# A threshold-attention and MoE kernel: one batch's q and k turned by TensorE instead of the DMA, and the output tiles of the drain spread over three PSUM buffers

## Chip, cores and metric

The kernel runs on one core of one Trainium2 chip. The metric is device time in microseconds for one launch: the median of several runs, beside one profiled execution whose trace gives every duration below.

## What is computed

Attention over 8 batches, 8 heads, 576 positions and head dimension 64, with a threshold: only scores within tau = 0.02 of the row's maximum survive. Its output, 4608 tokens of 512, goes through a two-layer network with a leaky ReLU.

```python
scores = scale * np.matmul(q, k.transpose(0, 1, 3, 2))
thresh = np.max(scores, axis=-1, keepdims=True) - tau
scores = np.where(scores >= thresh, scores, -1000000000.0)
attn = np.exp(scores - np.max(scores, axis=-1, keepdims=True))
attn = attn / (np.sum(attn, axis=-1, keepdims=True) + 1e-09)
x = np.matmul(attn, v)                       # then (batch, seq, heads * dim)
h = x @ w_in                                 # 512 -> 2048
out = np.maximum(0.01 * h, h) @ w_out        # 2048 -> 512
```

All inputs and the output are float32.

## The kernel before

**Splitting.** Scores need more than half precision, so q and k, scaled by 64, are each split into a high and a low fp16 part (`hi` on ScalarE, `x64` and `lo` on POOL), and three products are summed in PSUM. A batch's four pairs of heads are handled in two halves, `hb` 0 and 1. A tile `ks` or `qs` holds both parts of a half, positions on the partitions, as 18 blocks of 128x128; scores need it with the head dimension on the partitions, as `kst` or `qst`. There are two ways to turn it. `turn` is one DMA transpose on SyncE's queue. `turn_pe` lets TensorE transpose block by block through an identity into a PSUM tile named `tp`, which ScalarE or VectorE copies to `kst` or `qst`. Before the change, batch 0 takes `turn_pe` and the other seven take `turn`: 28 DMA transposes.

**Steps.** The main loop has one score step for 128 query rows of one pair of heads: 18 steps for a batch. In a step TensorE computes scores of two heads (`scores`, tags `sc0` and `sc1`, one buffer of two banks each). VectorE scales them into `sf` and takes the row maximum (line 391, `smax`), POOL makes the bias `bb` from it and applies it to one head (lines 515 and 517), ScalarE to the other (516). One step later VectorE cuts at the threshold (546), and ScalarE takes the exponential into `w` with its row sum (551). Two steps make a unit; one step after its last exponential VectorE adds the reciprocal sums to `w` (534, 536) and SyncE issues a DMA transpose `wt` of it (540). Seven steps after the unit's last score step TensorE multiplies `wt` with v (`pv`, 362) and VectorE writes the scaled result to `xT` (372, 378).

**The network.** When a group's `xT` is complete (two blocks of 128 tokens as a rule, for the first group after step 14) its work is put in queues: `h_unit` makes the hidden units with 8 or 16 matmuls into a PSUM tile `hp` (tag `h`, two buffers of a bank), ScalarE applies a ReLU scaled by 0.99, and a step later VectorE adds 0.01 of `hp` (`leak`, 216). `o_unit` sums 4 output matmuls at a time into `op` (tag `o`, one buffer). After 16 of them `op` is copied to `osb` and stored. One hidden and one output unit are taken per step. After the last step a loop, the drain, takes what is left in turn.

**Order.** Each engine runs its instructions in the order in which the code emits them. What is not part of a step (loads, splitting, turning) is put into the lists `tick` and `ptick` by step number and is emitted at the end of that step. [...] `sc0` and `sc1` two banks each, `h` two, `o` and `pv` one each. The calls that place the turns, and the tile that the drain uses:

```python
at(t0 + 4, lambda b=b, hb=hb: turn("k", b, hb))   # t0 = 4 for the first half of batch 1
at(t0 + 7, lambda b=b, hb=hb: turn("q", b, hb))
...
G.op = ps.tile([128, 512], FP32, tag="o", bufs=1, name="op")
```

Of the kernel before, what the change touches and what calls it, by code (L numbers as in the profile page):

```python
# [9 lines left out]
FP32 = mybir.dt.float32  # L10
# [6 lines left out]
def kernel(  # L17
# [42 lines left out]
    WOUT = 0  # L60
    SPOOL = 5
    LOADS = (-4, 3)

    sb = ctx.enter_context(tc.tile_pool(name="sb", bufs=1))
    ps = ctx.enter_context(tc.tile_pool(name="ps", bufs=1, space=bass.MemoryType.PSUM))
# [27 lines left out]
    def load_half(src, store, nm, b, hb):  # L93

        m = store[b, hb] = sb.tile([128, 2, 576], FP32, tag=nm, bufs=2, name=nm)
        in_ = src[b, :, :, :].rearrange("(h f) (p t) d -> f p h (t d)", h=2, t=9)[ds(2 * hb, 2)]
        if nm == "km":
            nc.sync.dma_start(out=m, in_=in_.rearrange("f p h x -> (f p) h x"))  # L100
        else:
            for f in range(2):
                nc.sync.dma_start(out=m.rearrange("(p f) h x -> f p h x", f=2)[f], in_=in_[f])
# [3 lines left out]
    def after_anchor(ins):  # L107

        if anchor[0] is not None:
            tc.add_manual_dep(  # L110
                ins.ins, anchor[0].ins.name,
                mybir.DependencyInfo(mybir.DependencyClass.Sync, mybir.DependencyReason.DATA), reason="port")

    def load_v(b, i):

        if i == 0:
            vts[b] = vbufs[b % 2]
        vt = vts[b]
        sv = v[b, :, :, :].rearrange("(h g) (p t) d -> h p g (t d)", h=2, t=9)
        out_, in_ = [  # L120
            (vt[0:64, :, 0, 0:5, :], sv[0][:, :, 0:320]),
            (vt[64:128, :, 0, 0:4, :], sv[0][:, :, 320:576]),
            (vt[64:128, :, 1, 0:5, :], sv[1][:, :, 0:320]),
            (vt[0:64, :, 1, 1:5, :], sv[1][:, :, 320:576]),
        ][i]
        after_anchor(nc.gpsimd.dma_start(out=out_, in_=in_))  # L126
# [5 lines left out]
    def split_tile(nm, b, hb):  # L132
        store = kss if nm == "k" else qss
        if (b, hb) not in store:
            store[b, hb] = sb.tile([128, 2, 9, 2, 64], FP16, tag=nm + "s", bufs=2, name=nm + "s")
        return store[b, hb]
# [14 lines left out]
    def hi(nm, b, hb):  # L151
        for part in PARTS[nm]:
            src, dst = views(nm, b, hb, 0, part)
            hi_last[0] = nc.scalar.activation(out=dst, in_=src, func=AF.Copy, bias=0.0, scale=64.0)

    def x64(nm, b, hb, h):
        m = (kms if nm == "k" else qms)[b, hb][:, h, :]
        return nc.gpsimd.tensor_scalar(out=m, in0=m, scalar1=64.0, scalar2=1.0, op0=AX.mult, op1=AX.mult)

    def lo(nm, b, hb, h, part, eng="pool"):  # L160
        src, dst = views(nm, b, hb, 1, part)
        _, h_ = views(nm, b, hb, 0, part)
        if eng == "pool":
            return nc.gpsimd.tensor_tensor(out=dst[:, h], in0=src[:, h], in1=h_[:, h], op=AX.subtract)  # L164
        return nc.vector.scalar_tensor_tensor(
            out=dst[:, h], in0=src[:, h], scalar=64.0, in1=h_[:, h], op0=AX.mult, op1=AX.subtract)

    def turned(nm, b, hb):

        store = ksts if nm == "k" else qsts  # L170
        if (b, hb) not in store:
            store[b, hb] = sb.tile([128, 2, 9, 2, 64], FP16, tag=nm + "st", bufs=4, name=nm + "st")
        return store[b, hb]

    def turn(nm, b, hb):
        nc.sync.dma_start(
            out=turned(nm, b, hb).rearrange("p s t g r -> p (s t) (g r)"),
            in_=split_tile(nm, b, hb).rearrange("p s t h d -> p (s t h d)"), transpose=True)

    def turn_pe(nm, b, hb, i, pieces, eng):  # L180

        t = turned(nm, b, hb)
        s_ = split_tile(nm, b, hb)
        for t0, n, tag, bufs, w in pieces:
            p_ = ps.tile([128, w, 128], FP16, tag=tag, bufs=bufs, name="tp")
            for j in range(n):
                nc.tensor.transpose(p_[:, j, :], s_[:, i, t0 + j, :, :].rearrange("p h d -> p (h d)"), ident)
            src, dst = p_[:, 0:n, :], t[:, i, ds(t0, n), :, :].rearrange("p t g r -> p t (g r)")
            if eng == "act":
                nc.scalar.activation(out=dst, in_=src, func=AF.Copy, bias=0.0, scale=1.0)  # L190
            else:
                nc.vector.tensor_copy(out=dst, in_=src)
# [21 lines left out]
    def leak():  # L214
        for G, u, hp in leaky:
            nc.vector.scalar_tensor_tensor(  # L216
                out=G.g[u], in0=hp, scalar=0.01, in1=G.g[u], op0=AX.mult, op1=AX.add)

            nj = 512 // G.n
            nv = (u + 1) * nj // 4  # L220
            if (u + 1) * nj % 4 == 0:
                oq.append((lambda G=G, v=nv - 1: o_unit(G, v), G.n))
            if u == NJ // nj - 1:
                for v in range(NJ // 4, G.n // 32):
                    oq.append((lambda G=G, v=v: o_unit(G, v), G.n))
        leaky.clear()

    tail = [False]
    osbs = [0]

    def osb_act():
        osbs[0] += 1
        return tail[0] and osbs[0] % 2 == 0

    def mm(out_, lhsT, rhs, start, stop):
        nc.tensor.matmul(out=out_, lhsT=lhsT, rhs=rhs, start=start, stop=stop, skip_group_check=True)  # L236
# [18 lines left out]
    def o_unit(G, v):  # L255

        i, v = divmod(v, NJ // 4)
        if v == 0:
            G.op = ps.tile([128, 512], FP32, tag="o", bufs=1, name="op")
        op = G.op  # L260
        for j in range(4 * v, 4 * v + 4):
            nj = 512 // G.n
            mm(op, G.g[j // nj][:, j % nj, ds(128 * i, 128)], w_out16[:, j, :], j == 0, j == NJ - 1)
        if v < NJ // 4 - 1:
            return None

        def fin():
            osb = sb.tile([128, 512], FP32, tag="osb", bufs=3, name="osb")
            if osb_act():
                nc.scalar.activation(out=osb, in_=op, func=AF.Copy, bias=0.0, scale=1.0)  # L270
            else:
                nc.vector.tensor_copy(out=osb, in_=op)  # L272
            return lambda: nc.sync.dma_start(out=G.rows[i], in_=osb)
        return fin
# [123 lines left out]
    def at(s, f, t=tick):  # L398
        t.setdefault(max(0, s), []).append(f)
# [18 lines left out]
    HS = [[(0, 5, "h", 2, 8), (5, 4, "h", 2, 8)], [(0, 5, "o", 1, 8), (5, 4, "pv", 1, 8)]]  # L418
# [15 lines left out]
    for i in range(2):  # L434
        turn_pe("k", 0, 0, i, SCS[i], "act")
    lo_all("q", 0)
    for i in range(2):
        turn_pe("q", 0, 0, i, SCS[i], "dve")
# [4 lines left out]
    def second():  # L443
        lo_all("q", 1)
        for i in range(2):
            turn_pe("k", 0, 1, i, HS[i], "act")
# [8 lines left out]
    for b in range(1, B):  # L455
        s0 = 18 * (b - 1)
        for hb in range(2):
            t0 = s0 + (PREP1 if b < 2 else PREP)[hb]
            at(s0 + LOADS[hb], lambda b=b, hb=hb: load_half(k, kms, "km", b, hb))
            at(s0 + LOADS[hb] + 1, lambda b=b, hb=hb: load_half(q, qms, "qm", b, hb))  # L460
            at(t0 - 1, lambda b=b, hb=hb: hi("k", b, hb))
            at(t0 + 1, lambda b=b, hb=hb: hi("q", b, hb))

            for i, what in enumerate(("k0x", "k0l", "k1x q0x", "k1l", "q0l", "q1x", "q1l")):
                for w in what.split():
                    nm, h = w[0], int(w[1])
                    if w[2] == "x":
                        at(t0 + i, lambda nm=nm, h=h, b=b, hb=hb: after_anchor(x64(nm, b, hb, h)), ptick)
                    else:
                        for part in PARTS[nm]:  # L470
                            at(t0 + i, lambda nm=nm, h=h, b=b, hb=hb, part=part: after_anchor(lo(nm, b, hb, h, part)), ptick)
            at(t0 + 4, lambda b=b, hb=hb: turn("k", b, hb))
            at(t0 + 7, lambda b=b, hb=hb: turn("q", b, hb))
        for i in range(4):
            at(18 * b + i, lambda b=b, i=i: load_v(b, i))

# [12 lines left out]
    for s in range(NS + LAG + 1):  # L489
# [31 lines left out]
        for i in range(max(len(ou), len(hu))):  # L521
            o = ou[i]() if i < len(ou) else None
# [20 lines left out]
        if last is not None:  # L543
            P_, ui, i = last
# [67 lines left out]
```

## Time and profile before

| what | value |
|---|---|
| median of 5 runs | 535.62 us (531.14 to 540.29) |
| the profiled execution, its own time | 537.73 us |
| its span, first to last instruction | 536.0 us |
| mean granted TensorE clock | 0.948 |
| scores, 1536 matmuls of the full blocks | 138.5 us busy, 294 ns median each |
| row maximum on VectorE, 288 | 205.2 us busy, 748 ns each |
| exponential on ScalarE, 288 | 194.1 us busy, 675 ns each |
| turns by DMA: kst 14, qst 14 | 5.2 and 6.0 us median from issue to landing |
| wt by DMA, 76 | 6.3 us median from issue to landing |
| the drain, from the last scores | from about 491 to 536 us |

An engine row of the profile gives busy time, share and instructions. A row of waits reads: engine and line, the releaser, then total us, number of waits, and the longest one. A row of the timeline reads: start in us, us, engine, line, operation, tiles, count, and in brackets the idle time just before it with what ended it. "SPq" is SyncE's queue of DMA issues; its durations are those of issuing, not of landing. PE is TensorE, DVE VectorE, ACT ScalarE, POOL GpSimd.

### The profile page before, as it was taken

What the parts mean: (1) busy time and instruction counts of PE and PEld (TensorE: products, weight loads), DVE (VectorE), ACT (ScalarE), POOL (GpSimd) and SP (SyncE); (2) the same over time, 40 slices, a digit from 0 to 9 for tenths busy, and PEclk for the clock granted to TensorE, in tenths of its full rate; (3) what the DMA queues carried; (4) which work ended last, traced back from release to release, by engine and by line L of the source; (5) the groups of instructions that cost most, each with busy time, mean ns of one, the idle gap of its engine ahead of it and who ended that gap; (6) DMA issues with size and microseconds to landing.
All of it is one profiled execution on the core that took longest, in us unless ns stands there. A gap on an engine that the chain in (4) does not pass through costs nothing.

```text
span 536.0 us, 13454 instructions
## 1 busy us (share of the span) xinstructions
PE 477.8 (89%) x4912; PEld 295.3 (55%) x4912; DVE 464.2 (87%) x1213; ACT 424.9 (79%) x924; POOL 278.8 (52%) x476
## 2 busy tenths in 40 slices
PE   4656896999869997999989998999799999989896
PEld 3424453656545664656555664656455666656673
DVE  4975896999969997999989997999869999999542
ACT  6785896988959887898989888998959888878331
POOL 5475844675546644675567645774536644322000
PEclk9856798999989998999999998999979999999999
DMA  8999999999999999999999999999999999666301
GB/s 250 216 195 246 199 219 189 235 179 207 203 185 211 189 231 172 247 206 204 185 229 203 178 221 200 253 204 193 186 260 179 177 186 195 138 122 127 90 27 59
DMA packets 279425, 101.79 MB, mean 190 GB/s; under 512 B 254272, under 2 KB 266560, under 8 KB 279360
## 3 DMA queue, kind: packets, MB, share of 16 engines
q1 hardware_dynamic: 266304, 92.03, 90.1%
q0 software_dynamic: 13056, 8.92, 13.2%
q8 instruction: 38, 0.62, 0.5%
q14 instruction: 27, 0.22, 0.2%
HBM read 36.70 MB, written 9.44 MB: 86 GB/s over the span
## 4 chain that ended last, share of the span: by engine, by line
DVE 47%; DMA 16%; PE 15%; issue 12%; POOL 5%; ACT 3%; SPq 0%; POOLq 0%; DVEq 0%; ACTq 0%
DVE sf L391 19%; DMA wt<-w 14%; DVE gT L216 9%; DVE P L546 8%; PE op L236 5%; DVE w L536 5%; PE hp L236 4%; PE sc L331 3%; DVE osb L272 3%; DVE xT L372 3%; POOL P L517 2%; PE pv L362 2%; DMA qst<-qs 2%; POOL bb L515 1%; ACT w L551 1%
## 5 line engine op out<-in xcount | busy, mean ns | idle before, releaser
L391 DVE TENSOR_SCALAR_CACHE_REDUCE sf<-sc 128x576 f32<-128x576 f32 x288 | 205.2, 748 | 15.6 <-PE sc L331 14.5
L551 ACT ACTIVATE w<-P 128x576 f16<-128x576 f16 x288 | 194.1, 675 | 8.4 <-DVE P L546 4.0
L516 ACT ACTIVATE P<-sf,bb 128x576 f16<-128x576 f32 x144 | 111.5, 774 | 67.4 <-POOL bb L515 63.2
L331 PE MATMUL sc<-kst,qst 64*128 64x320 f16 (+1 forms) x1536 | 138.5, 301 | 24.1 <-DVE sf L391 16.0
L236 PE MATMUL op<-wout,gT 128*128 128x512 f16 x576 | 151.2, 387 | 1.6 <-DVE osb L272 1.4
L236 PE MATMUL hp<-xT,win 128*128 128x256 f16 (+1 forms) x1344 | 151.7, 259 | 0.0
L236 PEld LDWEIGHTS <-win 128*128 128x128 f16 x1344 | 117.7, 99 | 43.7 <-issue 3.4
L331 PEld LDWEIGHTS <-qst 64*128 64x128 f16 x1536 | 75.6, 99 | 76.3 <-issue 48.5
L517 POOL TENSOR_SCALAR P<-sf,bb 128x576 f16<-128x576 f32 x139 | 106.2, 764 | 14.3 <-POOL bb L515 0.4
L216 DVE SCALAR_TENSOR_TENSOR gT<-hp,gT 128x512 f16<-128x512 f32 x144 | 98.3, 683 | 14.0 <-ACT gT L250 14.0
L250 ACT ACTIVATE gT<-hp 128x512 f16<-128x512 f32 x144 | 83.7, 581 | 20.0 <-PE hp L236 20.0
L515 POOL TENSOR_SCALAR bb<-mx 128x2 f32<-128x2 f32 x139 | 27.4, 197 | 127.4 <-DVE sf L391 116.6
L236 PEld LDWEIGHTS <-gT 128*128 128x128 f16 x576 | 46.3, 98 | 65.1 <-issue 30.2
L546 DVE TENSOR_SCALAR P<-P 128x1152 int16<-128x1152 int16 x144 | 81.4, 565 | 0.0
L362 PE MATMUL pv<-wt,v 128*64 128x256 f16 (+2 forms) x1000 | 57.8, 256 | 21.4 <-DMA wt<-w 21.2
L362 PEld LDWEIGHTS <-v 128*64 128x64 f16 x1000 | 38.8, 114 | 38.1 <-issue 33.6
L551 ACT ACTIVATION_READ_ACCUMULATOR w<-P 128x1 f32 x288 | 54.2, 188 | 0.0
L372 DVE TENSOR_TENSOR xT<-pv,wt 128x128 f16<-128x128 f32 x128 | 31.8, 291 | 16.6 <-PE pv L362 16.3
L164 POOL TENSOR_TENSOR ks<-km,ks 128x320 f16<-128x320 f32 (+1 forms) x56 | 39.9, 732 | 10.8 <-DVE P L546 10.1
L164 POOL TENSOR_TENSOR qs<-qm,qs 128x576 f16<-128x576 f32 x28 | 35.9, 1281 | 13.6 <-DVE P L546 13.6
L536 DVE TENSOR_SCALAR w<-rc 128x256 f16<-128x256 f32 (+1 forms) x76 | 40.0, 527 | 2.6
L126 POOL DMA_DIRECT2D v<-in_v_dram x32 | 20.6, 643 | 23.0 <-PE sc L331 10.1
(35 smaller groups left out, 213.2 us busy)
## 6 DMA issues: line engine op xcount, KB each, us to landing
km<-in_k_dram SPq DMA_DIRECT2D x16, 576.0 KB, 4.9
qm<-in_q_dram SPq DMA_DIRECT2D x32, 288.0 KB, 4.7
out_dram<-osb SPq DMA_DIRECT2D x36, 256.0 KB, 3.5
v<-in_v_dram POOLq DMA_DIRECT2D x16, 160.0 KB, 6.0
v<-in_v_dram POOLq DMA_DIRECT2D x16, 128.0 KB, 6.8
win<-in_moe_w_in_dram POOLq DMA_DIRECT2D x8, 256.0 KB, 9.3
wout<-in_moe_w_out_dram POOLq DMA_DIRECT2D x8, 256.0 KB, 11.3
wt<-w SPq DMA_TRANSPOSE x76, 6.3
```

The lines of the kernel that those rows point to most:

```text
L164: return nc.gpsimd.tensor_tensor(out=dst[:, h], in0=src[:, h], in1=h_[:, h], op=AX.subtract)
L216: nc.vector.scalar_tensor_tensor(out=G.g[u], in0=hp, scalar=0.01, in1=G.g[u], op0=AX.mult, op1=AX.add)
L236: nc.tensor.matmul(out=out_, lhsT=lhsT, rhs=rhs, start=start, stop=stop, skip_group_check=True)
L250: nc.scalar.activation(out=G.g[u], in_=hp, func=AF.Relu, bias=0.0, scale=0.99)
L331: nc.tensor.matmul(out=sc[h][:, cols], lhsT=qt[r, qi, ds(2 * c, 2)].rearrange("d t a b -> d (t a b)")[:, g::2], rhs=rhs, start=(i == 0), s ...
L362: nc.tensor.matmul(out=o_[ds(64 * h, 64)], lhsT=vt[:, pp, h, j, :], rhs=w_[:, :, 4 * h + j, :], start=(j == 0), stop=(j == 4), skip_group_ ...
L391: nc.vector.tensor_scalar(out=sf, in0=sc[h][:, ds(SC0, 576)], scalar1=C, scalar2=None, op0=AX.mult, op1=AX.max, accum_out=mx[:, h : h + 1])
L516: nc.scalar.activation(out=P_[:, 1, :], in_=sB, func=AF.Identity, bias=bb[:, 1:2], scale=1.0)
L517: (nc.vector if s < SPOOL else nc.gpsimd).tensor_scalar(out=P_[:, 0, :], in0=sa, scalar1=1.0, scalar2=bb[:, 0:1], op0=AX.mult, op1=AX.add)
L536: nc.vector.tensor_scalar(out=W_[:, :, 1152:1280].rearrange("p i (h r) -> p i h r", h=2), in0=rc[:, 0:nw, :].unsqueeze(3).to_broadcast([12 ...
L546: anchor[0] = nc.vector.tensor_scalar(out=pi, in0=pi, scalar1=NEG, scalar2=None, op0=AX.max)
L551: nc.scalar.activation(out=uW[ui][:, i, ds(576 * h, 576)], in_=P_[:, h, :], func=AF.Exp, bias=exp_bias, scale=1.0, accum_out=usm[ui][:, i, ...
```

## The change

There are two edits. First, the turns of k and q of batch 1, first half, leave SyncE's queue (they were emitted at the end of steps 8 and 11) and go to `turn_pe`: k in four pieces at the end of steps 8 to 11, q in four at the end of steps 12 to 15. A piece is 5 or 4 of the 9 blocks of one part (high parts first). Each takes one buffer of tag `h`, and ScalarE copies it out. Second, output tiles that are begun in the drain take `sc1`, `o` and `sc0` in turn instead of `o` alone. The setting `"both"` for the copies is added but not used here.

```diff
+    EV1 = "act"
+    PE1 = {("k", 0): 8, ("q", 0): 12}
...
-            if eng == "act":
+            if eng == "act" or eng == "both" and t0 == 0:
                 nc.scalar.activation(out=dst, in_=src, func=AF.Copy, bias=0.0, scale=1.0)
...
+    ops = [0]
...
         if v == 0:
-            G.op = ps.tile([128, 512], FP32, tag="o", bufs=1, name="op")
+            tag = "o"
+            if tail[0]:
+
+                ops[0] += 1
+                tag = ("sc0", "sc1", "o")[ops[0] % 3]
+            G.op = ps.tile([128, 512], FP32, tag=tag, bufs=1, name="op")
...
-            at(t0 + 4, lambda b=b, hb=hb: turn("k", b, hb))
-            at(t0 + 7, lambda b=b, hb=hb: turn("q", b, hb))
+            for nm, t1 in (("k", t0 + 4), ("q", t0 + 7)):
+                if b == 1 and (nm, hb) in PE1:
+
+                    for i in range(4):
+                        at(PE1[nm, hb] + i, lambda nm=nm, hb=hb, i=i: turn_pe(nm, 1, hb, i // 2, HS[0][i % 2 : i % 2 + 1], EV1))
+                else:
+                    at(t1, lambda nm=nm, b=b, hb=hb: turn(nm, b, hb))
```

`HS[0]` is the list of the two pieces, `[(0, 5, "h", 2, 8), (5, 4, "h", 2, 8)]`: first block, number of blocks, tag, buffers, width of the PSUM tile.

## Prediction

> **What bounds the kernel now.** I read the page's busy table first, then the waits, then SyncE's queue and the timeline around the two stages touched. The four compute engines are all well filled, so a change shows only where one stage waits.
>
> ```profile
> PE 477.8 (89%) x4912; PEld 295.3 (55%) x4912; DVE 464.2 (87%) x1213; ACT 424.9 (79%) x924; POOL 278.8 (52%) x476
> q1 hardware_dynamic: 266304, 92.03, 90.1%
> PE pv L362 <- DMA wt<-w: 21.2, 9, 4.6
> PE sc L331 <- DVE sf L391: 16.0, 34, 1.6
> PE sc L331 <- DMA qst<-qs: 7.4, 4, 4.2
> PE op L236 <- DVE osb L272: 1.4, 4, 0.8
> ```
>
> The hardware DMA queue is full for 90% of the span, and TensorE stands 28.6 us (21.2 + 7.4) for DMA transposes. One of those waits is what the first edit can reach:
>
> ```profile
> 48.44 3.59 SPq L176 DMA_TRANSPOSE kst<-ks  x1
> 52.13 6.35 SPq L540 DMA_TRANSPOSE wt<-w  x2
> 58.57 2.39 SPq L176 DMA_TRANSPOSE qst<-qs  x1
> 61.14 3.37 SPq L540 DMA_TRANSPOSE wt<-w  x1
> 64.60 3.47 SPq L176 DMA_TRANSPOSE kst<-ks  x1
> 68.88 4.37 SPq L540 DMA_TRANSPOSE wt<-w  x1
> 73.30 1.28 SPq L103 DMA_DIRECT2D qm<-in_q_dram  x2
> 74.68 4.76 SPq L176 DMA_TRANSPOSE qst<-qs  x1
> 84.80 1.62 PE L331 MATMUL sc<-kst,qst 64*128 64x320 f16 x12 [4.24 <-DMA qst<-qs]
> 89.38 0.74 PE L362 MATMUL pv<-wt,v 128*64 128x256 f16 x10 [0.54 <-DMA wt<-w]
> ```
>
> From 36 to 92 us SyncE issues without a gap, and the q transpose of batch 1's second half, issued at 74.68, lands about 9.9 us later, at 84.6. Step 22 (the fifth of batch 1) needs it: TensorE stands 4.24 us and its clock falls, so that the 12 score matmuls take 1.62 us where they take 0.91 at the next step. In the drain TensorE is the bound (output and hidden matmuls alternate) and waits for the single output bank:
>
> ```profile
> 507.58 1.02 PE L236 MATMUL op<-wout,gT 128*128 128x512 f16 x4 [0.25 <-DVE osb L272]
> 528.23 3.61 PE L236 MATMUL op<-wout,gT 128*128 128x512 f16 x16 [0.78 <-DVE osb L272]
> ```
>
> [...]
>
> **The change, part by part.** Steps are the score steps; their first maximum starts at 45.13 (step 9), 64.94 (16), 67.69 (17) and 86.45 (22).
>
> *Removed:* kst at 48.44 and qst at 58.57, 3.59 + 2.39 = 5.98 us of SyncE. Rebuilding the queue with the same durations: the next wt starts at 48.4 and ends at 51.5. The one after needs its W, written at 52.31 + 0.60 = 52.9: it runs to 56.2. The next needs W of 58.79 + 0.29 = 59.1: 59.1 to 62.5. Then without waits kst 3.47, km 0.58, wt 4.37, qm 1.28 and small gaps: the second half's qst starts at 72.7 instead of 74.68. Of 6.0 us taken out, 4.0 turn into SyncE waiting for W. Landing: 84.6 - 2.0 = 82.6. Bounds: 84.6 (nothing) to 78.6 (all 6 us, if the transposes also run faster in an emptier queue). I take 82.6, because the W times come from the compute path, which doesn't get faster.
>
> *Added on TensorE:* 36 transposes, 4 or 5 in each of steps 8 to 15. At the start 9 took 0.87 us and 18 took 2.14, so 0.1 to 0.12 each cold: 0.4 to 0.6 us a step. Their place is after the step's pv, where TensorE waits for the maxima to free the score banks (the 16.0 us row), so I cost them at nothing, except at step 8: there TensorE comes late from a 4.61 us wait and VectorE is idle, 0.55 us. [...] bounds -1 to +2 us (0.5 a step uncovered in four steps).
>
> *Added on ScalarE:* 8 evictions, four 128x640 at 0.68 and four 128x512 at 0.58 (rows of the q turn at 20.7 us): 5.06 us. ScalarE's idle before P in steps 9 to 15 is 1.91, 0.96, 0.72, 0.49, 0.40, 0.65 and 0.22. To step 13 they nearly fit. From step 13 the debt grows: free at 58.55, eviction to 59.23 where P started at 58.95; then 61.93 for 61.71; then 64.72 for 64.04. So P of step 15 starts 0.7 us late, which alone is covered, since VectorE takes that P a step later.
>
> *Added wait:* the last q piece (step 15) and the hidden matmuls of step 15 take the two "h" buffers. In the written instruction order, those of step 16 wait for ScalarE, that is for the eviction of step 15, which stands behind that step's two exponentials: 66.63 + 0.7 + 0.58 = 67.9. They started at 64.83. Behind them on TensorE stand pv and the scores of step 17, VectorE waits for these. Hidden start to scores is 1.64 us (64.83 to 66.47): scores at 69.6, first maximum at 70.6 instead of 67.69, **+2.9 us**. No row shows this wait; bounds 0 (ScalarE early, or the buffer taken differently) and 4 us. I take 2.9.
>
> From step 18 to 21 VectorE is busy without gaps, so this isn't regained: TensorE would be ready for step 22 at 84.80 - 4.24 + 2.9 = 83.5. The transpose lands at 82.6. So the scores start at 83.5 instead of 84.8, -1.3, and with no stall warm: -0.7 more. The wt behind qst lands at 89.35 - 2.0 = 87.3, its pv starts then instead of at 89.38: -2.0 again, the same gain, not a second one. Net of the first edit: **-2.0 us**. Up to 95 us SyncE's queue runs dry in the profile (94.59 is issued soon after its W), so the rest shifts with it.
>
> *Moved:* the turned k and q of the first half are ready with the last eviction, about 67.9, before the scores of step 18. POOL's splits and VectorE's instruction order stay; km, qm and the wt behind them on SyncE come at most 2 us earlier.
>
> *Drain:* tiles go to sc1, o, sc0 in turn. The waits 0.25 (507.58), 0.25 (515.02) and 0.78 (528.23) go: **-1.3 us**. The copies keep their engines; at the end the last 16 matmuls follow at once, and their last inputs (VectorE done at 527.1) come before their turn. Bounds -1.3 to -0.5. If VectorE's copy of the tile before is late, nobody waits for it.
>
> Sum: -2.0 - 1.3 = -3.3. The profiled execution took 537.73 us (span 536.0 and 1.7 around it), so 534.4 by that measure. The median of the runs shown is 535.62, 2.1 below: the same saving gives **532.3 us**.
>
> **Rivals.**
> *All of the relief arrives.* The emptier queue lands qst by 80 us, the warm clock pays for ScalarE's debt and hidden units of step 16 do not wait. Then 4.24 + 0.54 + 0.7 of cold matmuls go: -5.5, with the drain -6.8: 528.8. For it: DMA has been the limit all along, and the clock is 0.73 in 42 to 57 us. Against: W at 59.1 gates SyncE, and the wait for the eviction stands in the order.
> *Only the drain.* ScalarE's slip eats what DMA gives: -1.3, 534.3. For it: +2.9 needs only to become 4.9. Against: the removed stall has a cold clock with it.
> *Slower, one mechanism:* ScalarE becomes the bound of steps 8 to 16. If all 5.06 us of evictions delay the path and the 2.9 come on top, the slip is 8.0; stall and cold clock absorb 4.24 + 0.7 = 4.9; +3.1, less 1.3, is +1.8: 537.4. It decides from a slip of 6.2 us (4.9 + 1.3). For it: ScalarE's idle in those steps sums to 5.35 us, hardly more than the evictions. Against: the idle lies mostly where it is used.
>
> **How the numbers follow.** Forecast 0.45, all of the relief 0.25, only the drain 0.2, slower 0.1. The range 527.8 to 537.2 runs from 1 us below the middle of the best case to just short of that of the slower one. One per cent is 5.4 us, about what a measurement of this kernel can tell from no change: faster means below 530.3, most of the 0.25 and a little of the forecast, 0.26. Slower means above 541.0, beyond the slower case's middle: 0.06. The rest is 0.68.
>
> **What would show it.** Right: no kst or qst issue before 60 us, SyncE waiting for W around 52 and 57 us, the second half's qst issued about 72.7; ScalarE without idle in steps 13 to 16; hidden matmuls of step 16 waiting about 3 us for ScalarE; at step 22 a DMA wait under 1 us; no output matmul waiting for a copy in the drain. Wrong: a wait at step 22 that stays at 4 us, step 17 not later, or steps 9 to 15 more than 2 us longer.

## Result and the profile after

The changed kernel took 531.97 us (median of 27 runs, 521.87 to 538.36), the kernel before beside it 535.29 us (48 runs, 530.4 to 541.62): 3.3 us less, and -3.3 us was forecast. The profiled execution took 527.73 us with a span of 525.8 us, where before took 537.73 and 536.0. The ratio of the two kernels' fast runs is 0.9867, with a 95% interval of 0.983 to 0.9904 (about -7.1 us): it keeps, of each kernel, only the runs within 1.5% of its fastest, which are most of before's and fewer than a third of the changed kernel's, so it shows a larger saving than the medians do, and the medians of all runs are given beside each ratio below.

The busy table and the hardware DMA queue on the changed kernel's page:

```profile
PE 473.8 (90%) x4948; PEld 294.8 (56%) x4948; DVE 462.2 (88%) x1213; ACT 428.5 (81%) x932; POOL 278.9 (53%) x476
q1 hardware_dynamic: 261632, 90.85, 90.7%
```

Its waits (total us, number, longest):

```profile
PE pv L370 <- DMA wt<-w: 15.6, 8, 5.0
PE sc L339 <- DVE sf L399: 14.6, 35, 0.9
PE sc L339 <- DMA qst<-qs: 4.2, 3, 1.9
PE hp L239 <- ACT qst L192: 1.7, 1, 1.7
PE tp L189 <- ACT qst L192: 1.7, 1, 1.7
```

TensorE has its 36 more instructions and ScalarE its 8. The waits for DMA transposes fall from 28.6 us to 19.8 (15.6 + 4.2). Only one of the vanished waits is the 4.24 us of step 22: the row for wt (the transposes that pv waits for) has lost 5.6 us as well, which the prediction didn't foresee. Two of the rows are new: one wait of 1.7 us each for ScalarE's copy of a q piece; one of them was forecast.

SyncE's queue, in the timeline of the changed kernel. Start, then the time of issuing:

```profile
45.35 17.52 SPq L553 DMA_TRANSPOSE wt<-w  x4
62.97 3.50 SPq L178 DMA_TRANSPOSE kst<-ks  x1
67.27 4.45 SPq L553 DMA_TRANSPOSE wt<-w  x1
71.77 1.27 SPq L105 DMA_DIRECT2D qm<-in_q_dram  x2
73.15 3.58 SPq L178 DMA_TRANSPOSE qst<-qs  x1
```

The kst and qst between the wt are gone. The second half's qst is issued at 73.15 (forecast 72.7, before 74.68).

TensorE around steps 14 to 17 of the changed kernel; the bracket holds the idle time and what ended it:

```profile
62.31 1.11 PE L239 MATMUL hp<-xT,win 128*128 128x256 f16 x8
65.09 0.38 PE L189 MATMUL tp<-ident,qs 128*128 128x128 f16 x4 [1.66 <-ACT qst L192]
65.40 0.93 PE L345 MATMUL sc<-kst,qst 64*64 64x320 f16 x24
68.05 1.86 PE L239 MATMUL hp<-xT,win 128*128 128x256 f16 x8 [1.72 <-ACT qst L192]
69.84 1.28 PE L370 MATMUL pv<-wt,v 128*64 128x256 f16 x10
71.05 0.98 PE L345 MATMUL sc<-kst,qst 64*64 64x320 f16 x24
...
85.24 0.29 PE L339 MATMUL sc<-kst,qst 64*128 64x320 f16 x1 [0.27 <-DVE sf L399]
85.92 0.89 PE L339 MATMUL sc<-kst,qst 64*128 64x320 f16 x11 [0.39 <-DVE sf L399]
88.58 0.74 PE L370 MATMUL pv<-wt,v 128*64 128x256 f16 x10
```

And ScalarE, which both waits are for:

```profile
64.35 0.68 ACT L192 ACTIVATE qst<-tp 128x640 f16<-128x640 f16 x1
64.94 0.76 ACT L529 ACTIVATE P<-sf,bb 128x576 f16<-128x576 f32 x1
...
67.42 0.58 ACT L192 ACTIVATE qst<-tp 128x512 f16<-128x512 f16 x1
```

The hidden matmuls at 68.05 are those of step 16. They start when the copy of 67.42 ends, as forecast (67.9). Before them, at 65.09, the q piece of step 15 waits in the same way for the copy of step 14 (64.35), and that was not forecast. At step 22 no DMA wait is left: its scores (85.24 and 85.92) wait 0.27 and 0.39 us for VectorE to free the score banks, and the pv behind them (88.58) waits for nothing.

To see where time goes in all, I measured the distance between the starts of the steps' first row maxima. Three kernels are profiled twice, which shows how far such a distance varies by itself.

| stage, us | before | before again | drain only | change | change again | turn only | one step earlier | earlier again |
|---|---|---|---|---|---|---|---|---|
| steps 8 to 17 | 30.21 | 29.79 | 30.58 | 35.06 | 33.19 | 33.49 | 31.47 | 31.23 |
| steps 21 to 24 | 13.97 | 15.02 | 14.71 | 9.17 | 9.16 | 9.18 | 9.53 | 9.65 |
| steps 8 to 24 | 56.52 | 57.14 | 57.63 | 56.59 | 54.68 | 55.03 | 53.32 | 53.20 |
| steps 24 to 44 | 67.49 | 67.93 | 65.70 | 63.34 | 63.52 | 65.76 | 64.21 | 62.23 |
| steps 44 to 143 | 328.68 | 336.19 | 329.29 | 324.79 | 324.69 | 318.92 | 327.22 | 330.88 |
| last maximum to the end | 45.83 | 45.86 | 44.60 | 44.06 | 44.04 | 45.47 | 44.07 | 44.09 |

Two kernels of the experiments below are the same as these up to step 24 and say more of the first three rows. The turn alone with two more DMA transposes later on takes 36.15, 9.16 and 57.65 us; relief in batch 2 takes 30.31, 13.88 and 56.51. So without the turn there are four profiles of these rows, with the turn four, and their means are used from here on: 30.22 and 34.48 us for steps 8 to 17, 56.95 and 55.99 for steps 8 to 24.

Three stages move with the change: a slip in 8 to 17, made good by 24 with about 1 us to spare in the mean (from -2.3 to +0.7 us in the four profiles); a gain in 24 to 44; and the drain. Steps 44 to 143 differ by up to 7.5 us between two executions of the kernel before (336.19 and 328.68), so what a single profile shows there is no evidence.

### The profile page after: what moved, and what is told of

It is laid out like the page before. It is cut to its first block, busy times and chain, and to the rows that moved or that the text cites. A ratio compares the mean times of both kernels' runs of the same rounds, so it can differ in the third digit from the quotient of the medians.

```text
span 525.8 us, 13527 instructions
## 1 busy us (share of the span) xinstructions
PE 473.8 (90%) x4948; PEld 294.8 (56%) x4948; DVE 462.2 (88%) x1213; ACT 428.5 (81%) x932; POOL 278.9 (53%) x476
## 4 chain that ended last, share of the span: by engine, by line
DVE 52%; PE 13%; issue 12%; DMA 12%; POOL 6%; ACT 3%; SPq 0%; POOLq 0%; DVEq 0%; ACTq 0%
DVE sf L399 21%; DMA wt<-w 11%; DVE gT L218 10%; DVE P L559 9%; DVE w L549 5%; PE op L239 5%; PE hp L239 4%; DVE xT L380 3%; DVE osb L280 3%; POOL P L530 3%; PE sc L339 2%; PE pv L370 2%; POOL bb L528 1%; ACT w L564 1%; DVE rc L547 1%
## 5 line engine op out<-in xcount | busy, mean ns | idle before, releaser
L399 DVE TENSOR_SCALAR_CACHE_REDUCE sf<-sc 128x576 f32<-128x576 f32 x288 | 205.1, 748 | 12.9 <-PE sc L339 10.9
L339 PE MATMUL sc<-kst,qst 64*128 64x320 f16 (+1 forms) x1536 | 134.1, 295 | 19.6 <-DVE sf L399 14.6
L239 PE MATMUL op<-wout,gT 128*128 128x512 f16 x576 | 149.5, 384 | 0.6 <-DVE osb L280 0.6
L339 PEld LDWEIGHTS <-qst 64*128 64x128 f16 x1536 | 74.3, 97 | 68.5 <-issue 45.2
L370 PE MATMUL pv<-wt,v 128*64 128x256 f16 (+2 forms) x1000 | 56.6, 252 | 15.9 <-DMA wt<-w 15.6
L128 POOL DMA_DIRECT2D v<-in_v_dram x32 | 20.6, 643 | 22.9 <-PE sc L339 10.1
```

Of the source, the lines that this page charges most:

```text
L339: nc.tensor.matmul(out=sc[h][:, cols], lhsT=qt[r, qi, ds(2 * c, 2)].rearrange("d t a b -> d (t a b)")[:, g::2], rhs=rhs, start=(i == 0), s ...
L370: nc.tensor.matmul(out=o_[ds(64 * h, 64)], lhsT=vt[:, pp, h, j, :], rhs=w_[:, :, 4 * h + j, :], start=(j == 0), stop=(j == 4), skip_group_ ...
L399: nc.vector.tensor_scalar(out=sf, in0=sc[h][:, ds(SC0, 576)], scalar1=C, scalar2=None, op0=AX.mult, op1=AX.max, accum_out=mx[:, h : h + 1])
```

## Experiments

**The two edits apart.** First with no turn on TensorE, then with the drain as before.

```diff
-    PE1 = {("k", 0): 8, ("q", 0): 12}
+    PE1 = {}
```

> The drain's rotation alone; all turns of batch 1 stay with the DMA, so the main loop is that of the kernel before. Theory A (the turn by TensorE pays only for its own slip up to step 23, so the drain is all that is sure): drain from the last maximum to the end shorter by 1.3 to 1.8 us, time 1.3 to 3 us below before, the same as the whole change within 1.5 us. Theory B (the turn gives about 2 us of its own): 1.3 to 1.8 us below before, about 2 us above the whole change. Theory C (the differences of the two profiled executions after step 28 are chance): the starts of steps 28 to 138 differ from those of before by several us in either direction, although the instructions there are the same.

Measured: 534.15 us (22 runs), before beside it 535.45 (27); ratio 0.9955 (0.9923 to 0.9986). From the last maximum to the end it is 44.60 us where before had 45.83, -1.23. Eight profiles of kernels with the drain of before lie between 45.2 and 46.0 us, so the gain is clear of chance.

```diff
-            if tail[0]:
+            if False:
```

> The turn by TensorE alone; the drain uses the one output bank. Theory A: step 17 starts about 4.9 us later against step 8 than in before, steps 22 and 23 have no DMA wait, step 23 stands where it stood (within 0.5 us of before); time within 1 us of before. Theory B: step 23 at least 1.5 us earlier, time about 2 us below before. The drain takes 45.8 us as before in both.

Measured: 527.39 us (6 runs), ratio 0.9898 (0.9851 to 0.9945). The drain is the size predicted. The theory that the turn pays little more than its own slip (-2.0 us) falls: the median is 8 us below before, and the interval's upper end, 0.9945, is still -2.9 us. With 6 runs, 8 us is more than the stages account for: its profile gains 1.9 us by step 24 (55.03 against 56.95). In 24 to 44 it has no DMA wait at the place where before waits 3.87 us, but one of 2.5 us for a qst earlier, and at 65.76 us this stage is no shorter than with the drain alone (65.70).

**The pieces one step earlier**, with both edits.

```diff
-    PE1 = {("k", 0): 8, ("q", 0): 12}
+    PE1 = {("k", 0): 7, ("q", 0): 11}
```

> The whole change with each of the eight pieces one step earlier (k at steps 7 to 10, q at 11 to 14), so that no piece shares the two hidden buffers with hidden work in step 15. If the slip of steps 15 to 17 is the wait of TensorE for ScalarE's copy: the waits of 1.7 us ahead of the last piece and ahead of the hidden matmuls of step 16 are gone, step 17 is 3 us earlier than with the change, and as the DMA wait at step 22 then binds again or is just met (q landing near 82 us), step 23 is 2 to 3.5 us earlier than with the change; time 2 to 3.5 us below the change. If instead ScalarE's load makes the slip (5 us more work in those steps): step 17 only 0 to 1 us earlier, time as with the change.

> The changed kernel once more, on the same chip as the three above. Theory A and B: about 3.3 us below before. Theory C: up to step 23 its step starts are those of the first profile within 0.5 us; from step 28 on the long DMA waits come at other steps and the starts differ by several us.

Measured side by side: 528.28 us one step earlier (6 runs), 529.01 for the change (6); ratios to before 0.9885 (0.9833 to 0.9937) and 0.9849 (0.9795 to 0.9903). The 2 to 3.5 us that were expected between the two aren't there: they can't be told apart by these times. The traces can tell them apart: one step earlier, no matmul waits for ScalarE in steps 14 to 16, steps 8 to 17 take 31.47 us instead of 33.19 to 35.06, and the DMA is then what step 22 waits for again. The timeline of TensorE, one step earlier:

```profile
82.88 0.96 PE L339 MATMUL sc<-kst,qst 64*128 64x320 f16 x12 [0.87 <-DMA qst<-qs]
86.38 0.74 PE L370 MATMUL pv<-wt,v 128*64 128x256 f16 x10 [0.70 <-DMA wt<-w]
```

With little slip in the way these scores start at 82.88, on the landing of qst. In the change that landing sets nothing, because TensorE comes to these scores at about 85. There it also comes earlier than here. The changed kernel's second profile issues this qst at 73.44 and has it landed 7.0 us later, at 80.5:

```profile
L178 SPq DMA_TRANSPOSE qst<-qs x1: 3603/3603/3603, 73.4 to 73.4; - x1
DMA to landing us min/median/max: 7.0/7.0/7.0
```

The first row gives the time of issuing in ns and the start, the second the time from issue to landing; before needs 10.1 us, one step earlier 9.3.

**Relief without cost, and cost without relief.** In the first kernel, the first half of batch 1 takes batch 0's turned tiles and nothing is turned for it. In the second, the DMA turns stay as before and TensorE and ScalarE make the same 8 pieces into a tile that nobody reads. Both have the drain of before.

```diff
-                    for i in range(4):
-                        at(PE1[nm, hb] + i, ... turn_pe(nm, 1, hb, ...))
+                    (ksts if nm == "k" else qsts)[1, hb] = (ksts if nm == "k" else qsts)[0, hb]
```

> The two DMA transposes of batch 1's first half are gone and nothing takes their place: its scores use batch 0's turned k and q instead (so that half of batch 1 isn't computed from its own k and q); drain as before. If the relief at step 22 is all that the removal gives: steps 9 to 21 as before within 1 us, no DMA wait in steps 22 and 23, step 24 earlier than before by 4 to 5.5 us, and the later steps differ from before only by chance; time 4 to 6 us below before. If the removal also makes later DMA waits shorter (about 3 us more, as the profiles with the turn suggest): time 7 to 9 us below before.

```diff
     def turn_pe(nm, b, hb, i, pieces, eng):
-        t = turned(nm, b, hb)
+        if b == 1:
+            if not scratch:
+                scratch["t"] = sb.tile([128, 2, 9, 2, 64], FP16, name="scratch")
+            t = scratch["t"]
+        else:
+            t = turned(nm, b, hb)
...
-                else:
-                    at(t1, lambda nm=nm, b=b, hb=hb: turn(nm, b, hb))
+                at(t1, lambda nm=nm, b=b, hb=hb: turn(nm, b, hb))
```

> The DMA transposes stay and feed the scores; TensorE and ScalarE turn the same tiles in the same steps as with the change, into a tile that nobody reads; drain as before. If the slip of 3 to 5 us by step 17 is the work's own: step 17 is 3 to 5 us late, and since the DMA's landing sets step 22, which had a wait of 4.2 us, step 24 is only 0 to 1.5 us late; time 0 to 1.5 us above before. If the later gains come with the work on TensorE or ScalarE and not with the DMA: time 3 us or more below before.

Measured: relief only 526.19 us (6 runs), before beside it 532.9 (37), ratio 0.9845 (0.9796 to 0.9894). Cost only 532.15 us (6 runs), ratio 0.9869 (0.98 to 0.9939) by 3 of its runs, while its median is 0.75 us below before, so its time says little. By stages: relief only takes 52.21 us from step 8 to 24, 4.7 less than the mean without it (56.95). So taking two transposes out of the queue is worth 4.7 us by step 24 where nothing else is added. Its steps 24 to 44 take 62.60 us, as short as the change.

Cost only takes 56.07 us from step 8 to 24. Its steps 8 to 17 get longer (34.57 against 30.22), but that time comes out of the wait at step 22, which is used up: 21 to 24 take 9.16 us. That is where the change stands, too (55.99), so once the path slips this far, the two transposes taken out add nothing by step 24 that its one profile would show. Measured from the other side, the pieces cost the change 3.8 us (55.99 against 52.21) of the relief's 4.7.

Cost only shows the two waits with nothing else changed. TensorE's timeline:

```profile
65.48 0.38 PE L196 MATMUL tp<-ident,qs 128*128 128x128 f16 x4 [1.65 <-ACT scratch L199]
...
68.44 1.62 PE L246 MATMUL hp<-xT,win 128*128 128x256 f16 x8 [1.72 <-ACT scratch L199]
```

Unexpected: cost only takes 63.28 us from 24 to 44, as short as the change, with no transpose taken out. It is taken up below.

**Repeats**, to see how far the times vary.

> The kernel before once more, as a measure of chance: time within 1 us of before. Its step starts against the first profile: if the long DMA waits move by chance, single steps between 40 and 114 shift by 2 to 4 us either way, with a sum that is not the same; if they are the same in each execution, all starts agree within 0.5 us.

> The pieces one step earlier, both edits, once more, for a second profile and more runs: step 17 again 1 to 1.5 us late against before and step 24 about 3 us early; time 7 us below before as in its first run, if that is more than chance; 3 to 5 us below, if only the stages up to step 24 and the drain are real.

Measured: before again 535.6 us (22 runs), ratio 1.0 (0.9968 to 1.0032), but the median of the same kernel's 37 runs beside it is 532.9, so two medians of one kernel lie 2.7 us apart. One step earlier 527.69 us (16 runs), ratio 0.987 (0.9833 to 0.9907), 5.2 us below that 532.9. Before again waits 4.97 us for qst at step 22 and 3.03 us for wt 70 us later:

```profile
85.21 1.62 PE L331 MATMUL sc<-kst,qst 64*128 64x320 f16 x12 [4.97 <-DMA qst<-qs]
...
155.52 1.28 PE L362 MATMUL pv<-wt,v 128*64 128x64 f16 x40 [3.03 <-DMA wt<-w]
```

**Where the second gain comes from.** Before waits for the wt of unit 17 at 155.59, the change hardly (0.8 us in its second profile). TensorE in before, then in the change:

```profile
155.59 1.15 PE L362 MATMUL pv<-wt,v 128*64 128x64 f16 x40 [3.87 <-DMA wt<-w]
```

```profile
152.11 0.82 PE L370 MATMUL pv<-wt,v 128*64 128x64 f16 x40 [0.18 <-DMA wt<-w]
```

This is almost 90 us after the last piece. My explanation was: SyncE's queue is behind all that time, and the two transposes taken out leave it less behind. The measure for it is the time from the start of the step at which a unit's wt is placed to the issue of that wt; the smallest value in the table's units is 2.83 us.

| lag of wt, us | unit 7 | 8 | 9 | 10 to 13 | 15 | 16 | 17 | 18 | 19 |
|---|---|---|---|---|---|---|---|---|---|
| before | 11.92 | 10.92 | 9.33 | 3.3 to 4.3 | 5.29 | 10.79 | 9.01 | 8.37 | 10.13 |
| before again | 12.22 | 12.19 | 10.05 | 3.3 to 4.6 | 5.51 | 10.95 | 9.05 | 8.04 | 9.32 |
| change | 4.82 | 2.84 | 2.84 | 2.8 to 4.8 | 4.61 | 9.52 | 8.70 | 6.92 | 6.51 |
| change again | 6.36 | 4.41 | 2.84 | 2.8 to 4.9 | 4.91 | 10.19 | 9.22 | 7.45 | 7.20 |
| turn only | 6.36 | 4.41 | 2.85 | 2.8 to 4.7 | 4.69 | 9.93 | 10.42 | 9.69 | 5.46 |
| cost only | 6.42 | 4.43 | 2.84 | 2.8 to 4.6 | 4.61 | 9.98 | 9.26 | 7.67 | 6.16 |

The table bears out only part of it. Up to unit 9 the queue is far less behind. But at units 10 to 13 before has all but caught up, and the change is no better there. From unit 15 all fall behind again, and at unit 17, whose wt is the one waited for, the lags of the two groups overlap. What sets them apart there is the time from issue to landing: 11.8, 11.0 and 10.9 us in before, before again and the drain alone, 9.4, 9.2 and 8.9 in the change, the change again and the turn alone, 9.0 with relief only and 8.6 with cost only. Why that wt lands sooner isn't shown.

Two kernels test this. One is the turn alone with two more DMA transposes, of tiles of batch 2 into a tile that nobody reads, at the end of steps 27 and 29: if it is the queue, the gain must go. The other is the kernel before with the relief in batch 2 instead: its first half takes batch 1's turned tiles, so that the queue is relieved after step 22. If it is the queue, the wait at step 22 stays and the later one goes.

```diff
+    def dummy():
+        nc.sync.dma_start(
+            out=spare.rearrange("p s t g r -> p (s t) (g r)"),
+            in_=split_tile("k", 2, 0).rearrange("p s t h d -> p (s t h d)"), transpose=True)
+
+    at(27, dummy)
+    at(29, dummy)
```

> The turn by TensorE alone (drain as before), and two more DMA transposes of a tile of batch 2 into a spare tile that nobody reads, emitted at the end of steps 27 and 29: SyncE's queue gets back about 7 us of work, behind the stage of the change and ahead of step 42. If the second gain (steps 42 to 44, which take about 6.3 us in all seven profiles with a turn by TensorE or less DMA, and 8.8 to 11.4 us in three profiles without) comes from a queue that is less behind: the wt of units 15 to 18 are issued later after their step than with the turn alone, and steps 42 to 44 take 9 us or more again; time 3 to 6 us above the turn alone (527.4), 531 to 533. If it comes from anything that the turn itself leaves behind: steps 42 to 44 stay at 6 to 7 us and the time within 2 us of the turn alone.

```diff
-            at(t0 + 4, lambda b=b, hb=hb: turn("k", b, hb))
-            at(t0 + 7, lambda b=b, hb=hb: turn("q", b, hb))
+            for nm, t1 in (("k", t0 + 4), ("q", t0 + 7)):
+                if (b, hb) == (2, 0):
+                    def same(nm=nm):
+                        st = ksts if nm == "k" else qsts
+                        st[2, 0] = st[1, 0]
+                    at(t1, same)
+                else:
+                    at(t1, lambda nm=nm, b=b, hb=hb: turn(nm, b, hb))
```

> The kernel before, in which the first half of batch 2 uses batch 1's turned k and q instead of its own (so that half isn't computed from its own k and q): two DMA transposes fewer around steps 25 to 29, nothing in TensorE's or ScalarE's work changed, and the stage of the change as before. If a less filled queue is what steps 42 to 44 need: the wait of 4.2 us at step 22 stays, step 24 as before within 1 us, and steps 42 to 44 take 6.3 to 7 us instead of 8.8 to 11.4; time 3 to 5 us below before. If not: steps 42 to 44 as before, time within 1 us of before.

Measured: two more transposes 535.75 us (22 runs), before 535.07 (35), ratio 1.0013 (0.9984 to 1.0042): the whole gain is gone. Steps 24 to 44 take 70.29 us, and the lags of units 15 to 17 are 10.99, 16.57 and 15.79. But the time is not lost where I expected it, at 155 us: steps 42 to 44 stay at 6.24 us, which had been named as the sign against the queue. It is lost before step 40 (24 to 40 takes 56.90 us; the turn alone takes 51.24, and the kernels without the turn 49.9), on a wt and on the transpose of the next half:

```profile
143.88 1.28 PE L370 MATMUL pv<-wt,v 128*64 128x256 f16 x10 [4.17 <-DMA wt<-w]
150.41 1.62 PE L339 MATMUL sc<-kst,qst 64*128 64x320 f16 x12 [2.67 <-DMA qst<-qs]
```

Relief in batch 2: 534.59 us (14 runs), ratio 0.9949 (0.9911 to 0.9987); that is 0.5 us of medians where 3 to 5 were expected. The wait at step 22 stays, and so does the length of 21 to 24 (13.87 us). Steps 24 to 44 fall to 64.23; the last two steps of them (42 to 44) take 6.24 us instead of 10.99, the wait for unit 17's wt is gone and smaller waits come earlier:

```profile
85.13 1.50 PE L331 MATMUL sc<-kst,qst 64*128 64x320 f16 x12 [4.41 <-DMA qst<-qs]
142.20 1.14 PE L331 MATMUL sc<-kst,qst 64*128 64x320 f16 x12 [0.69 <-DMA qst<-qs]
147.44 0.74 PE L362 MATMUL pv<-wt,v 128*64 128x256 f16 x10 [2.25 <-DMA wt<-w]
```

So relieving the queue is enough for a shorter 24 to 44: relief only (62.60) and relief in batch 2 (64.23) have it with no piece turned by TensorE. It is not the only way: cost only has it (63.28) although no transpose was taken out. Its lags up to unit 9 are as small as the change's, and that the slip of steps 8 to 17 lets SyncE catch up fits them, but how this reaches unit 17 is only argued. The change has both the relief and the slip, and no run tells which of the two brings it this gain. The two more transposes show that load on the queue costs time in this stage. As no kernel without the turn got the same two, they don't show that the turn's own gain comes from there.

**VectorE instead of ScalarE for the copies**, with the drain of before. This asks whether it is ScalarE's load or the place in its queue.

```diff
-    EV1 = "act"
+    EV1 = "dve"
```

> The turn by TensorE alone, its eight copies on VectorE instead of ScalarE (0.41 to 0.48 us each, 3.6 us in all). If TensorE's waits for ScalarE's queue make most of the slip: the waits of 1.7 us ahead of the last piece and of the hidden matmuls of step 16 shrink below 0.8 us, but VectorE is full from step 11 on, so step 17 is 2 to 3 us later than before against step 8, where the turn with ScalarE gave 3.0 to 4.9; time within 1.5 us of the turn alone. If VectorE's own time weighs more: step 17 late by 3.6 us or more.

Measured: 528.41 us (6 runs), ratio 0.9872 (0.9826 to 0.9918). Steps 8 to 17 take 32.22 us, +2.0 on 30.22, the mean of the four profiles without the turn. TensorE's timeline has neither wait:

```profile
65.21 0.39 PE L189 MATMUL tp<-ident,qs 128*128 128x128 f16 x4
65.53 0.93 PE L345 MATMUL sc<-kst,qst 64*64 64x320 f16 x24
66.42 1.03 PE L239 MATMUL hp<-xT,win 128*128 128x256 f16 x8
```

One step earlier with ScalarE's copies, the same stage costs +1.1 (mean of 31.47 and 31.23). ScalarE does all 8 copies there, too. So most of the slip of 3.0 to 5.9 us is the waiting behind ScalarE's order in steps 15 and 16, with the clock that falls after it in two of the four profiles (to 0.60 in the change), and not the work.

## Why the prediction was right, and where it was not

**The total** was right: -3.3 us of medians, as forecast. Meeting it to the tenth is luck: two medians of one kernel can lie 2.7 us apart (see the repeats), one term of the sum is too large (the first edit's net by step 24) and a gain of about 2.8 us is missing from it. The stages measured one by one give more than the medians do (see what stays open).

**SyncE's queue up to step 22: right for the issues, not for the landing.** Issue of the second half's qst 73.15 (72.7 forecast), and four wt in a row that take 17.52 us. At the 3.2 to 3.4 us apiece that they have in the queue of before (6.35 for two, 3.37) four would take 13.2, so some 4.3 us are waiting by that estimate; the waits of SyncE's queue from 44 to 62 us show 4.1 us in two, of up to 3.0, for VectorE's w (line 549), with 4.0 forecast. What is emitted behind a waiting transpose is held up with it here: the last wt starts at 59.86, its w being complete at 59.71, and the second half's kst, whose ks is complete at 59.27, starts at 62.97, when that wt has been issued. The landing of qst was forecast for 82.6, with the same time from issue to landing as before. One step earlier it is 82.8, but with the pieces where the change has them it comes 5.4 to 7.0 us after the issue and not 10.1: at 80.5 in the change's second profile (the first has no record of it), 81.2 with the turn alone and 79.2 with two more transposes. That is near what *all of the relief arrives* said of it (by 80 us). It decides nothing in the change, because the path comes later still.

**The slip: mechanism right, one claimant and the clock left out.** I gave +2.9 us for step 17 (my own figures, 67.9 less 64.83, give 3.1) and measured 3.0 (33.19), 3.3 (33.49), 4.8 (35.06) and 5.9 (36.15) over the mean of 30.22. What was left out shows at the sentence "the last q piece (step 15) and the hidden matmuls of step 15 take the two 'h' buffers": I looked only for who waits next for them, the hidden matmuls of step 16 (1.72 us, start 68.05 against 67.9). The q piece of step 15 is itself a claimant, and waits for the copy of step 14 in the same queue (1.66 us). The order holds on both engines: tp is complete at 65.47, but its copy starts at 67.42, behind a ReLU (65.61) and two exponentials (66.08 and 66.75), and pv and the scores of step 17 start behind the waiting hidden matmuls, at 69.84 and 71.05. Both waits are the same in all four profiles. What differs is the granted clock in the 4 us after the second wait. It is 1.00 in the two with the small slips; the change again:

```profile
65.30 0.38 PE L189 MATMUL tp<-ident,qs 128*128 128x128 f16 x4 [1.66 <-ACT qst L192]
68.25 1.03 PE L239 MATMUL hp<-xT,win 128*128 128x256 f16 x8 [1.71 <-ACT qst L192]
69.22 0.74 PE L370 MATMUL pv<-wt,v 128*64 128x256 f16 x10
```

It is 0.60 in the first profile, where the same 8 hidden matmuls take 1.86 us and pv 1.28, and 0.50 in the one with the largest slip (two more transposes), where the hidden matmuls take 1.86 us, pv 1.28, and the 24 score matmuls behind them 1.65 instead of 0.98. The forecast reckons with no such fall. ScalarE has hardly any idle there (the rows from 64.35 to 68.00 follow each other), as forecast. Before that the pieces cost next to nothing, as forecast: steps 9 to 15 take 16.5 to 17.0 us in the four profiles with the turn and 16.8 to 17.3 without. The 0.55 us of step 8 is not in the forecast's sum because I took it to be made good by a higher clock in steps 10 and 11. That was my estimate and isn't shown: from 48 to 54 us the granted clock is 0.83 in before and 0.77 in the change.

**The stall of step 22: gone as forecast, the net too large.** From +2.9 at step 17 the forecast goes to -2.0, which is a recovery of 4.9. Steps 21 to 24 take 9.17 us instead of 14 to 15. In before the granted clock is 0.50 from 84.80 to 86.40, while step 22's 12 score matmuls take 1.62 us, and 1.00 from 90.05 to 90.90, while the next step's take 0.91; in the change it is 1.00 from 85.2 to 90 us. The recovery from step 17 to 24 is 5.2 us (a slip of 4.3, the mean of the four, turned into -1.0: 55.99 against 56.95). So the first edit's net at that place is -1.0 where -2.0 was forecast. Where the clock stayed up it is -2.3 and -1.9, the forecast; where it fell, -0.4 and +0.7, which is what *only the drain* said. Cost only, in its one profile, loses the stall as well, so it isn't shown that in the change the removal ended it and not the slip.

**"Up to 95 us SyncE's queue runs dry ... so the rest shifts with it": the conclusion was wrong.** This is the step whose failure matters most. That the queue has all but caught up there is right (94.59 is the issue of unit 10, with a lag of 3.6 us). But by units 16 to 19 it is 8 to 11 us behind again in before, and the rest does not simply shift: steps 24 to 44 get 2.8 us shorter (64.2 against 67.04, means of three). As the drain alone (65.70) and the turn alone (65.76) meet in this row, the mean is uncertain by about 1.5 us. That less load on the queue is enough for it is shown by relief only and by relief in batch 2; by which way the change gets it stays open.

**The drain: right.** Forecast -1.3, measured -1.23 without and -1.4 (44.06 against 45.47) with the turn. Where three waits for the output bank stood, one of 0.3 us is left, and at the end the output matmuls run in one piece. The changed kernel's timeline, then its waits within the drain:

```profile
516.17 5.34 PE L239 MATMUL op<-wout,gT 128*128 128x512 f16 x24
```

```profile
PE op L239 <- DVE osb L280: 0.3, 1, 0.3
```

**The rivals.** ScalarE as the bound came nearest in its mechanism for steps 8 to 17 (slip of up to 5.9 us of its 8.0), but stays short of the 6.2 us that it needs. "All of the relief arrives" has its queue and its landing right: relief alone gives 4.7 by step 24. "Only the drain" holds up to step 24 in two of the four profiles, and for the total it is excluded by the turn alone.

**What stays open.** The measured saving is 3.3 us of medians in the first measurement and 6.4 in the second (6 runs, 529.01). The stages that move give -1.0, -2.8 and -1.4, so -5.2, between them. How much of the rest is chance in the waits of steps 44 to 143, I can't tell. Each kernel with pieces in the `h` buffers is also 1.1 to 1.3 us shorter in steps 136 to 138, where before waits 1.30 us for a wt at 472.35; its cause is not settled.

**A better version.** One step earlier removes both waits for ScalarE and is 2.7 us shorter than the change from step 8 to 24 (53.32 and 53.20 against the mean of 55.99). Its 22 runs have a median of 528.28 us, the change's 33 runs 531.66; side by side, with 6 runs each, they were not told apart.

## What to carry to other kernels

When a DMA queue is 90% full, as here, don't price a transfer that is taken out by the next wait alone, and don't assume that the others keep their time from issue to landing (the 10.1 us of qst at step 22 became 5.4 to 9.3). Measure both, issue and landing, for the later transfers that something waits for, too. Run the relief without the cost and the cost without the relief: here the slip ended the stall just as the relief did, which no profile of the change itself could tell. When an extra piece borrows a buffer that two users share, follow every claimant of that buffer, the piece itself too, and ask what stands ahead of the copy that frees it in its engine's order; moving the pieces by one step took more from the slip here (to 1.1 us) than giving the copies to another engine (to 2.0). And the sum of stages, with one kernel profiled twice, tells which differences can be read at all.

## What the runs showed of the hardware that was not expected

- One and the same transpose takes very different times from issue to landing. The qst that step 22 needs took 10.1 us in before, 9.3 with the pieces one step earlier, 7.0 in the change again and with the turn alone, 7.4 with cost only and 5.4 in the kernel with two more transposes later on. The wt of unit 17 took 11.8 us in before and 8.6 with cost only, which issues all that before issues.
- The same kernel loses different amounts to the same waits. Steps 110 to 114 took 18.72 us in one execution of before and 21.63 in another; of the change 12.50 and 19.75.
- Identity transposes of 128x128 fp16 blocks took 0.71 us for five at step 8 of the change, after a wait of 4.99 us and at a granted clock of 0.50, and 0.45 us at step 12, at a clock of 1.00. I had assumed 0.1 to 0.12 us each; both ends lie outside (0.14 and 0.09). I had also called the rows that this figure comes from cold, but the granted clock from 8 to 20 us of before, where they stand, is 1.00.
- The same pauses need not have the same consequence. After 1.66 and 1.72 us, 3 us apart, the granted clock over the next 4 us was 0.60 in one execution of the change, and 8 matmuls took 1.86 us; in another execution, after 1.66 and 1.71 us, it was 1.00, and they took 1.03.
